# The decay products over all 128 rows of PE, with zeros in the selection matrix, in a three-stage kernel

## The chip, the cores and the metric

The kernel runs on one core of one Trainium2 chip. The metric is the device time of one execution in microseconds, lower is better. The median of three timed runs of the kernel before is 510.32 us (509.98 to 510.88). One execution was taken by the hardware profiler.

## The reference

Three stages follow one another: a chunked linear attention over 4 batches of 8 heads with 768 steps, then two layers of 8 experts that send each of 3072 tokens to one expert. The change touches the attention alone. Cut to what matters there:

```python
for c in range(nc):                       # chunks of the sequence
    la = log_a[:, :, sl]
    cum = np.cumsum(la, axis=-1)
    L = np.exp(cum[:, :, :, None] - cum[:, :, None, :]) * causal
    M = np.einsum('bhin,bhjn->bhij', Cc, Bc) * L
    y_intra = np.einsum('bhij,bhjd->bhid', M, xc)
    y_inter = np.einsum('bhin,bhnd->bhid', Cc, state) * np.exp(cum)[..., None]
    y[:, :, sl] = y_intra + y_inter
    state = decay_full * state + np.sum(Bx * decay_from_j, axis=2)
...
x = _moe_ref(x=x, **moe_kwargs)
return _moe2_ref(x=x, **moe2_kwargs)
```

`L` holds the decay products: for steps i and j of a chunk, the product of all `a` between them.

## The kernel before

The attention is cut into chunks of 64 steps (12 in a sequence) and eight quads `q`, a quad being four heads of a batch. Every engine has its own queue and runs it in order; the queues are filled in the order in which the program is written, and waits are put in wherever an instruction reads or overwrites what another engine writes or reads.

The decay products are made by a scan on DVE (line 580) along a row of `a`. The row has to stand on all 64 partitions of a head's chunk, so PE spreads it: `decay_piece(b, g, v)` (line 570) multiplies a selection matrix `selA` (ones in the row of the head, zeros elsewhere) by `asp`, which holds `a` of all 32 batch-and-head rows. To keep the precision of 32 bits `a` is split in a high part (rows 0 to 31) and the rest (rows 32 to 63), and the product adds both. Two matmuls of 256 columns, called a pair here, fill one PSUM tile `ab`. The products use only rows 0 to 63 of PE (`tile_position=(0, 0)`). Rows 64 to 127 of the same two tiles serve another purpose: there `asp` holds the running product from a chunk's start, and `selA` in its first 512 columns a selection for it, which `quad_p` (line 685) multiplies on rows 64 to 127 of PE (tile `pp`, 384 columns, one matmul for each quad).

`asp` is written in two steps. Rows 0 to 63 are written near the start (`a_part`, lines 861 to 864). Rows 64 to 127 are written in `chunk_start` (line 897): DVE scans `ac` (line 903), ACT casts the result into `asp[64:128]` (line 907), and a later DVE subtraction puts the rest into `asp[96:128]` (line 913). Between those two the program has `pend.intra(1)`.

A generator (`filler`, line 618) gives out the steps in a fixed order: for each pair of chunks `k` the product `cb` of C and B (line 603, two 32-bit matmuls of 256 columns, each recorded as two), and then one `decay_piece`. `psA`, the PSUM pool that `ab` and `cb` share, has two buffers. While batch 0 is worked on, `need` (line 653) puts a matmul `pw` on zeros of 512 columns (line 651) behind each step; these are the fillers. `quad_intra` (line 711) makes the `y` products with 64-column weights from the finished masks `mb` (line 610, DVE).

At the program's start POOL clears the buffers that SP's loads fill in part (`cw`, which holds the three `ctm`, and `xbd`); SP issues the loads in order, so a load that waits for a clear holds those behind it.

Of the kernel before, what the change touches and what calls it, by code (L numbers as in the profile page):

```python
# [9 lines left out]
F32 = mybir.dt.float32  # L10
F32R = mybir.dt.float32r
# [8 lines left out]
NB, NH, S, HD, NS = 4, 8, 768, 32, 16  # L20
NTOK, D, E, F = NB * S, 256, 8, 1024
CH = 64
# [14 lines left out]
def ssm_moe_moe_kernel(  # L37
# [20 lines left out]
    pe, dve, act, pool, sp = nc.tensor, nc.vector, nc.scalar, nc.gpsimd, nc.sync  # L58
# [461 lines left out]
    with ExitStack() as actx:  # L520
# [3 lines left out]
        ab = actx.enter_context(tc.tile_pool(name="ab", bufs=1))  # L524
# [45 lines left out]
        def decay_piece(b, g, v):  # L570

            if v == 0:
                lts[b, g] = fil_p.tile([128, 4, 4, CH], F32, tag="lt", name=f"lt{b}_{g}", bufs=3)
            p = psA.tile([128, 512], F32, tag="a", name=f"ab{b}_{g}_{v}")
            for k in range(2):
                u = 4 * b + 2 * v + k
                pe.matmul(p[:, 256 * k:256 * k + 256], lhsT=selA[0:64, 128 * u:128 * u + 128],  # L577
                          rhs=asp[0:64, 256 * g:256 * g + 256], start=True, stop=True,
                          tile_position=(0, 0))
            dve.tensor_tensor_scan(  # L580
                lts[b, g][:, 2 * v:2 * v + 2].rearrange("p u c i -> p (u c i)"), p,
                ipat[:].rearrange("p c i -> p (c i)"), 0.0, op0=ALU.mult, op1=ALU.add,
            )
            if v == 1:
                lt = lts[b, g]
                for hq in range(2):
                    m = au.tile([128, 2, 4, 80], F32, tag=f"mb{hq}", name=f"mb{b}_{g}_{hq}",
                                bufs=5 + hq)
                    mbs[2 * b + hq, g] = m
                    us_ = slice(2 * hq, 2 * hq + 2)  # L590
                    pool.tensor_tensor(  # L591
                        m[:, :, :, 64:80], brs[b][:, us_, 4 * g:4 * g + 4],
                        lt[:, us_, :, CH - 1:CH].to_broadcast([128, 2, 4, NS]), ALU.mult,
                    )
# [23 lines left out]
        def filler():  # L618
            for b in range(NB):
                if b == 0:  # L620
                    for v in range(2):
                        decay_piece(0, 0, v)
                        yield
                for k in range(6):
                    yield from cb_steps(b, k)
                    fpos[b] = 2 * k + 1
                    yield
                    gb, gg = divmod(3 * b + k // 2 + 1, 3)
                    if gb < NB:
                        decay_piece(gb, gg, k % 2)  # L630
                        yield
# [14 lines left out]
        def warm(n):  # L646

            nwarm[0] += 1
            p = psC.tile([128, 512], F32, tag="c", name=f"pw{nwarm[0]}")
            for _ in range(n):  # L650
                pe.matmul(p, lhsT=wz[:, :128], rhs=wz, start=True, stop=True)

        def need(b, c):
            while fpos.get(b, -1) < c:
                if next(fil_gen, "end") == "end":
                    return
                if b == 0:
                    warm(1)
# [26 lines left out]
        def quad_p(q):  # L685

            b, hq = divmod(q, 2)
            p = psC.tile([128, 512], F32, tag="c", name=f"pp{q}")
            pe.matmul(p[:, :384], lhsT=selA[64:128, 128 * b:128 * b + 128],
                      rhs=asp[64:128, 384 * hq:384 * hq + 384], start=True, stop=True,  # L690
                      tile_position=(64, 0))
            pv = p[:, :384].rearrange("p (v i) -> p v i", i=CH)
            if q == NQ - 2:
                return pv
            t = au.tile([128, 6, CH], F32, tag="pt", name=f"pt{q}")
            act.copy(t, pv)
            return t
# [113 lines left out]
        def run(gen, n=None):  # L811
# [17 lines left out]
            out=ident, in_=ident, compare_op=ALU.not_equal, fill=1.0, base=0,  # L829
            pattern=[[-1, 128]], channel_multiplier=1,  # L830
        )
        pool.memset(ctm[0][:, :2], 0.0)
        pool.memset(ctm[1], 0.0)
        xbd = [ab.tile([128, NCH, 64], F32, name=f"xbd{i}") for i in range(4)]
# [11 lines left out]
        dve.tensor_reduce(idk, ident[:].rearrange("p (b k) -> p k b", k=32), axis=AX.X, op=ALU.add)  # L846
        hm = ab.tile([128, 2], F32, name="hm")
        dve.tensor_reduce(hm, idk[:].rearrange("p (h n) -> p h n", n=16), axis=AX.X, op=ALU.add)
        selA = ab.tile([128, 32 * CH], F32R, name="selA")
        asp = ab.tile([128, S], F32R, name="asp")  # L850

        def sel_part(b):
            hs = slice(8 * b, 8 * b + 8)
            act.copy(
                selA[0:64, 512 * b:512 * b + 512].rearrange("p (h j) -> p h j", j=CH),
                idk[0:64, hs].unsqueeze(2).to_broadcast([64, 8, CH]),
            )
# [9 lines left out]
        a_part(0, 256)  # L867
        a_part(256, S)
        sel_part(0)
        ipat = const.tile([128, 8, CH], F32, name="ipat")  # L870
        cxs = {0: load_cx(0), 1: load_cx(1)}
# [104 lines left out]
        pend = Quad(0)  # L976
        pend.intra(0)
        sel_part(1)
        halves[2] = expand_half(2, raws[2])
        xts[1] = expand_x(1, xcs[1], act.copy)  # L980
# [7 lines left out]
        for q in range(4):  # L988
# [2 lines left out]
        need(0, 7)  # L991
        pool.memset(cxb[0], 0.0)
        need(0, 11)
        act.copy(
            selA[64:128, :512].rearrange("p (h n) -> p h n", n=NS),
            idk[64:128].unsqueeze(2).to_broadcast([64, 32, NS]),
        )
        halves[3] = expand_half(3, raws[3])
# [15 lines left out]
        for b in range(2, NB):  # L1014
            sel_part(b)
# [11 lines left out]
        for q in range(1, NQ - 2):  # L1027
            b, hq = divmod(q, 2)
# [3 lines left out]
            if q == 1:  # L1032
                prefill(scr1, R1, [(C1P, C1T)], range(4))
                pts[0] = quad_p(0)
                for r in range(4):
                    quad_c(0, r)
                warm(2)
                fil(1)
                run(cs)
                warm(2)  # L1040
                pend.fb = quad_f(0)
            sx = quad_state(q - 1, pend.us, pend.fb)
            cur.intra(0)
            fil(1)
            pts[q] = quad_p(q)
            pend.ss = quad_transpose(q - 1, sx)
            fil(1)
# [46 lines left out]
        c6.intra(1)  # L1094
        run(router, 1)
        pts[q] = quad_p(q)
        run(router, 1)
        pend.ss = quad_transpose(q - 1, sx)
# [221 lines left out]
    for e in range(E):  # L1320
# [6 lines left out]
        for f in range(KF):  # L1327
# [3 lines left out]
            if nxr is not None and f in (4, 6):  # L1331
# [3 lines left out]
        n = nc.values_load(cnt2[0:1, e:e + 1], min_val=0, max_val=NTOK + NE,  # L1335
                           skip_runtime_bounds_check_because="counts of tokens")
# [80 lines left out]
```

## Time and profile before

| | us |
|---|---|
| median of three timed runs | 510.32 |
| the profiled execution, its own time | 506.59 |
| its span, first to last instruction | 504.9 |
| PE busy | 461.8 |
| DVE busy | 287.9 |
| ACT busy | 240.1 |
| POOL busy | 138.2 |
| attention and routing, up to the first expert's matmuls | about 143 |

Busy times are those of an engine's instructions in the profiled execution, whose span is 1.7 us shorter than its own time. PE's clock has two levels, 1.2 and 2.4 GHz; the granted clock of a stretch is a mean of the two, as a share of the higher one. PE is followed by its weight loads as an engine of its own (PEld), since these run beside matmuls. The start of a matmul is recorded, and its end is worked out by the profiler, so the distances between starts are the ones to read.

### The profile page before, as it was taken

How to read it: one execution, taken by the hardware profiler on the slowest of the kernel's cores; microseconds unless marked ns; L12 is line 12 of the kernel's file. 1: busy time of each engine (PE TensorE's matmuls, PEld its weight loads, DVE VectorE, ACT ScalarE, POOL GpSimd, SP SyncE). 2: the span in 40 equal slices, each digit the busy share in tenths (PEclk: the TensorE clock that was granted, in tenths of full speed). 3: DMA queues.
4: the chain of work that ended last, by engine and by line, in shares of the span. 5: the costliest groups of instructions: out<-in, count | busy, mean ns of one | idle time of the engine just before them, and what ended most of it. 6: DMA issues, size and time to landing. Idle time of an engine off the chain costs nothing.

```text
span 504.9 us, 8965 instructions
## 1 busy us (share of the span) xinstructions
PE 461.8 (91%) x3208; PEld 413.7 (82%) x3208; DVE 287.9 (57%) x681; ACT 240.1 (48%) x557; POOL 138.2 (27%) x210
## 2 busy tenths in 40 slices
PE   8889987988579999999999999879999999999992
PEld 3555755767569999999999999879999999999991
DVE  7877786877545836547373656533675367244330
ACT  5542443656435644637354465424566356344330
POOL 6334455156730021230303122411101210212011
PEclk9897998989959999999999999889999999999997
DMA  7257899785224535253443444260654564411000
GB/s 261 68 170 183 229 209 249 169 273 194 80 84 166 176 106 183 93 159 105 140 149 113 150 143 164 73 204 30 225 179 162 174 206 154 143 34 63 22 23 15
DMA packets 50226, 72.22 MB, mean 143 GB/s; under 512 B 23870, under 2 KB 36093, under 8 KB 49899
## 3 DMA queue, kind: packets, MB, share of 16 engines
q1 hardware_dynamic: 45595, 61.66, 41.3%
q0 software_dynamic: 4560, 9.70, 5.7%
q8 instruction: 34, 0.56, 0.5%
q14 instruction: 37, 0.30, 0.2%
HBM read 52.53 MB, written 19.74 MB: 143 GB/s over the span
## 4 chain that ended last, share of the span: by engine, by line
PE 47%; DMA 22%; issue 13%; DVE 9%; POOL 3%; ACT 2%; SPq 1%; POOLq 1%; another core or an unknown queue 0%; DVEq 0%; ACTq 0%
DMA out_dram<-os0n,idsn 13%; PE y1m L330 7%; PE y0m L330 7%; DMA out_dram<-os0n0a,idsn0a 7%; PE cb L603 3%; DVE lt L580 2%; PE h0m L308 2%; PE h1m L308 2%; PE h2m L308 2%; PE y L758 2%; PE h3m L308 2%; PE h6m L308 2%; PE h5m L308 2%; PE h7m L308 2%; PE h4m L308 2%
## 5 line engine op out<-in xcount | busy, mean ns | idle before, releaser
L218 POOL DMA_INDIRECT scr<-rows2m,idxm x31 | 31.4, 1014 | 128.7 <-DVE cum L215 105.3
L121 DVE TENSOR_TENSOR w0l<-raw,w0h 128x1024 fp32r<-128x1024 f32 x30 | 36.7, 1225 | 10.7 <-ACT w0h L120 10.7
L121 DVE TENSOR_TENSOR w1l<-raw,w1h 128x1024 fp32r<-128x1024 f32 x30 | 36.4, 1216 | 1.0 <-ACT w1h L120 1.0
L603 PE MATMUL cb<-cw,btt 128*128 128x256 f32 x96 | 31.6, 435 | 1.4 <-DVE mb L610 0.9
L437 POOL DMA_INDIRECT out_dram<-os0n,idsn x8 | 7.8, 969 | 89.1 <-ACT os0n L436 55.8
L218 POOL DMA_INDIRECT scr<-rows,idxa x24 | 26.3, 1094 | 20.3 <-DVE cum L215 10.3
L120 ACT CAST w1h<-raw 128x1024 fp32r<-128x1024 f32 x30 | 31.5, 1052 | 0.0
L120 ACT CAST w0h<-raw 128x1024 fp32r<-128x1024 f32 x30 | 31.2, 1042 | 0.0
L580 DVE TENSOR_TENSOR_SCAN lt<-ab,ipat 128x512 f32<-128x512 f32 x24 | 29.2, 1217 | 2.2 <-PE ab L577 2.0
L312 DVE SCALAR_TENSOR_TENSOR hln<-h0n,hhn 128x384 fp32r<-128x384 f32 (+1 forms) x8 | 4.2, 524 | 45.4 <-ACT hhn L311 41.5
L603 PEld LDWEIGHTS cb<-cw,btt 128*128 128x128 f32 x96 | 17.9, 209 | 9.2 <-issue 2.2
L610 DVE TENSOR_TENSOR mb<-cb,lt 128x256 f32<-128x256 f32 x48 | 18.0, 416 | 11.4 <-PE cb L603 9.4
L330 PE MATMUL y1m<-hhm,w1h 128*128 128x432 f32 (+1 forms) x64 | 23.0, 360 | 0.0
L330 PE MATMUL y0m<-hhm,w1h 128*128 128x432 f32 (+1 forms) x64 | 22.9, 358 | 0.0
L312 DVE SCALAR_TENSOR_TENSOR hlm<-h0m,hhm 128x432 fp32r<-128x432 f32 (+1 forms) x8 | 4.7, 586 | 31.4 <-ACT hhm L311 24.4
L330 PE MATMUL y0m<-hhm,w1l 128*128 128x432 f32 (+1 forms) x64 | 22.4, 350 | 0.0
L330 PE MATMUL y1m<-hhm,w1l 128*128 128x432 f32 (+1 forms) x64 | 22.3, 349 | 0.0
L330 PE MATMUL y0m<-hlm,w1h 128*128 128x432 f32 (+1 forms) x64 | 22.3, 348 | 0.0
L330 PE MATMUL y1m<-hlm,w1h 128*128 128x432 f32 (+1 forms) x64 | 22.3, 348 | 0.0
L591 POOL TENSOR_TENSOR mb<-brt,lt 128x128 f32<-128x128 f32 x24 | 10.5, 438 | 38.8 <-DVE lt L580 34.4
L715 PEld LDWEIGHTS y<-mb,xbd 128*64 128x64 f32 x384 | 14.8, 138 | 5.7 <-issue 2.0
L335 ACT COPY ytm<-y1m 128x432 f32<-128x432 f32 (+1 forms) x8 | 4.0, 502 | 31.8 <-PE y1m L330 31.8
(603 smaller groups left out, 1579.0 us busy)
## 6 DMA issues: line engine op xcount, KB each, us to landing
raw<-in_m2w_dram SPq DMA_DIRECT2D x32, 512.0 KB
raw<-in_m1w_dram SPq DMA_DIRECT2D x28, 512.0 KB
scr<-zrow SPq DMA_DIRECT2D x8, 448.9 KB
scr<-zrow SPq DMA_DIRECT2D x8, 399.0 KB
xrm<-scr SPq DMA_DIRECT2D x7, 448.9 KB
xrn<-scr SPq DMA_DIRECT2D x6, 399.0 KB
xbd<-in_xs__dram SPq DMA_DIRECT2D x24, 96.0 KB
scr<-zrow SPq DMA_DIRECT2D x8, 266.0 KB
```

What stands on the lines that cost most here:

```text
L120: act.copy(hi[:, sl], raw)
L121: dve.tensor_tensor(lo[:, sl], raw, hi[:, sl].bitcast(F32), ALU.subtract)
L218: i = pool.indirect_dma_start(out=scr[:], out_offset=bass.IndirectOffsetOnAxis(ap=idx[:pn, t, :], axis=0), in_=rows[:, t, :W], in_offset=None,
L308: pe.matmul(p[:, :n], lhsT=w[:, o:o + 128], rhs=x[:, kd, :n], start=(k == 0), stop=(k == 5))
L312: dve.scalar_tensor_tensor(hl[:, f, :n], p[:, :n], 0.0, hh[:, f, :n].bitcast(F32), op0=ALU.max, op1=ALU.subtract,)
L330: pe.matmul(p[:, :n], lhsT=w[:, o:o + 128], rhs=h[:, f, :n], start=(k == 0), stop=(k == 3 * KF - 1))
L580: dve.tensor_tensor_scan(lts[b, g][:, 2 * v:2 * v + 2].rearrange("p u c i -> p (u c i)"), p, ipat[:].rearrange("p c i -> p (c i)"), 0.0, o ...
L591: pool.tensor_tensor(m[:, :, :, 64:80], brs[b][:, us_, 4 * g:4 * g + 4], lt[:, us_, :, CH - 1:CH].to_broadcast([128, 2, 4, NS]), ALU.mult,)
L603: pe.matmul(p[:, cc], lhsT=btt[:, c].rearrange("p h j -> p (h j)"), rhs=ctt[:, :, c * CH:(c + 1) * CH], start=True, stop=True)
L610: dve.tensor_tensor(mbs[2 * b + hq, g][:, :, o:o + 2, :64].rearrange("p u c i -> p c u i"), p[:, :, us_, :], lts[b, g][:, us_, o:o + 2, :] ...
L715: pe.matmul(yps[g][64 * hs:64 * hs + 64, r * 80:r * 80 + 80], lhsT=xts[hs][:, c, :], rhs=mbs[q, c // 4][:, hs, c % 4, :], start=(r == 0), ...
L758: pe.matmul(yps[g][64 * hs:64 * hs + 64, :320].rearrange("p (c w) -> p c w", w=80)[:, :n, :64], lhsT=ss[:, g, 64 * hs:64 * hs + 64], rhs=c ...
```

## The change

The decay products and `pp` are no longer made on half of the rows of PE. The selection of `pp` moves out of `selA` into a tile of its own, `selP`, with zeros in rows 0 to 63. Rows 64 to 127 of `selA` become zeros, so that a product over all 128 rows has the same value. POOL clears those rows, and at the start also `asp[64:128]`, which is read before its values are written. The numbers of instructions on PE, DVE, ACT and SP stay as they were; POOL gets six clears more.

```diff
--- before.py
+++ after.py
@@ -574,9 +574,8 @@
             p = psA.tile([128, 512], F32, tag="a", name=f"ab{b}_{g}_{v}")
             for k in range(2):
                 u = 4 * b + 2 * v + k
-                pe.matmul(p[:, 256 * k:256 * k + 256], lhsT=selA[0:64, 128 * u:128 * u + 128],
-                          rhs=asp[0:64, 256 * g:256 * g + 256], start=True, stop=True,
-                          tile_position=(0, 0))
+                pe.matmul(p[:, 256 * k:256 * k + 256], lhsT=selA[:, 128 * u:128 * u + 128],
+                          rhs=asp[:, 256 * g:256 * g + 256], start=True, stop=True)
             dve.tensor_tensor_scan(
                 lts[b, g][:, 2 * v:2 * v + 2].rearrange("p u c i -> p (u c i)"), p,
                 ipat[:].rearrange("p c i -> p (c i)"), 0.0, op0=ALU.mult, op1=ALU.add,
@@ -686,9 +685,8 @@
 
             b, hq = divmod(q, 2)
             p = psC.tile([128, 512], F32, tag="c", name=f"pp{q}")
-            pe.matmul(p[:, :384], lhsT=selA[64:128, 128 * b:128 * b + 128],
-                      rhs=asp[64:128, 384 * hq:384 * hq + 384], start=True, stop=True,
-                      tile_position=(64, 0))
+            pe.matmul(p[:, :384], lhsT=selP[:, 128 * b:128 * b + 128],
+                      rhs=asp[:, 384 * hq:384 * hq + 384], start=True, stop=True)
             pv = p[:, :384].rearrange("p (v i) -> p v i", i=CH)
             if q == NQ - 2:
                 return pv
@@ -829,6 +827,10 @@
             out=ident, in_=ident, compare_op=ALU.not_equal, fill=1.0, base=0,
             pattern=[[-1, 128]], channel_multiplier=1,
         )
+        selA = ab.tile([128, 32 * CH], F32R, name="selA")
+        asp = ab.tile([128, S], F32R, name="asp")
+        pool.memset(selA[64:128, :512].bitcast(F32), 0.0)
+        pool.memset(asp[64:128].bitcast(F32), 0.0)
         pool.memset(ctm[0][:, :2], 0.0)
         pool.memset(ctm[1], 0.0)
         xbd = [ab.tile([128, NCH, 64], F32, name=f"xbd{i}") for i in range(4)]
@@ -846,11 +848,12 @@
         dve.tensor_reduce(idk, ident[:].rearrange("p (b k) -> p k b", k=32), axis=AX.X, op=ALU.add)
         hm = ab.tile([128, 2], F32, name="hm")
         dve.tensor_reduce(hm, idk[:].rearrange("p (h n) -> p h n", n=16), axis=AX.X, op=ALU.add)
-        selA = ab.tile([128, 32 * CH], F32R, name="selA")
-        asp = ab.tile([128, S], F32R, name="asp")
+        selP = ab.tile([128, 4 * 128], F32R, name="selP")
 
         def sel_part(b):
             hs = slice(8 * b, 8 * b + 8)
+            if b:
+                pool.memset(selA[64:128, 512 * b:512 * b + 512].bitcast(F32), 0.0)
             act.copy(
                 selA[0:64, 512 * b:512 * b + 512].rearrange("p (h j) -> p h j", j=CH),
                 idk[0:64, hs].unsqueeze(2).to_broadcast([64, 8, CH]),
@@ -991,8 +994,9 @@
         need(0, 7)
         pool.memset(cxb[0], 0.0)
         need(0, 11)
+        pool.memset(selP[0:64].bitcast(F32), 0.0)
         act.copy(
-            selA[64:128, :512].rearrange("p (h n) -> p h n", n=NS),
+            selP[64:128].rearrange("p (h n) -> p h n", n=NS),
             idk[64:128].unsqueeze(2).to_broadcast([64, 32, NS]),
         )
         halves[3] = expand_half(3, raws[3])
```

On PE, in batch 0 behind the first `y` products, stands the third decay piece (tile `ab_2_0`; `pw` is a filler, `cb_3` the product of chunk pair 3). Before:

```order
L715 MATMUL y_0_242<-mb_1_0_258,xbd_121 64x80
L577 MATMUL ab_2_0_307<-asp,selA 128x256 x2
L651 LDWEIGHTS wz
L651 MATMUL pw_311<-wz 128x512 [waits PE_49]
L603 MATMUL cb_3_313<-cw,btt_208 128x256 [waits DMAHW1_49,DMAHW2_49,DMAHW0_49,DMAHW3_49,DVE_49,PE_49]
```

And now:

```order
L713 MATMUL y_0_245<-mb_1_0_261,xbd_125 64x80
L577 MATMUL ab_2_0_311<-asp,selA 128x256 [waits Activation_49]
L577 MATMUL ab_2_0_311<-asp,selA 128x256
L650 LDWEIGHTS wz
L650 MATMUL pw_315<-wz 128x512 [waits PE_49]
L602 MATMUL cb_3_317<-cw,btt_211 128x256 [waits DMAHW1_49,DMAHW2_49,DMAHW0_49,DMAHW3_49,DVE_49,PE_49]
```

The order is the same, but the pair now waits for ACT, whose queue has these rows up to the cast into the upper half of `asp` (the last but one):

```order
L722 COPY us_243<-y_0_245 128x16x4
L857 CAST selA<-idk 64x512
L548 ACTIVATE btt_287<-btr_233,hm 128x6x64 x2
L667 COPY xbd_126<-xc_187 64x12x32 x2
L667 COPY xbd_127<-xc_187 64x12x32 x2
L985 CAST sel<-idk 64x1024
L910 CAST asp<-ac 64x768
L914 CAST fp<-fc 64x12
```

This queue is as it was before, and its first row still waits for the `y` product of PE that stands ahead of the pair.

On POOL, at the program's start, the queue was this:

```order
L828 AFFINE_SELECT ident<-ident 128x128
L832 MEMSET cw 128x768
L833 MEMSET cw 128x1536
L837 MEMSET xbd_120 128x768
L837 MEMSET xbd_121 128x768
```

And is now this:

```order
L826 AFFINE_SELECT ident<-ident 128x128
L832 MEMSET selA 64x512
L833 MEMSET asp 64x768
L834 MEMSET cw 128x768
L835 MEMSET cw 128x1536
L839 MEMSET xbd_124 128x768
L839 MEMSET xbd_125 128x768
```

Two clears stand ahead of those of `cw`, for which SP's loads wait.

## Rows read from the trace of the kernel before

**Rows 1.** The page's head and its row of granted clock, 40 slices of the span.

```profile
span 504.9 us, 8965 instructions
...
PEclk9897998989959999999999999889999999999997
```

**Rows 2.** Stretches: length, busy us of PE, PEld, DVE, ACT, POOL, clock, DMA.

```profile
21.00:24.00 3.00, 3.00 (x23) 1.71 (x22) 1.52 (x4) 0.23 (x3) 2.27 (x11) 0.66 0.00 0
...
37.00:44.00 7.00, 7.00 (x21) 4.02 (x22) 3.94 (x7) 2.49 (x7) 4.62 (x6) 0.54 0.69 172
...
62.00:85.00 23.00, 17.34 (x172) 11.92 (x173) 18.48 (x42) 9.97 (x35) 14.39 (x18) 0.99 1.03 223
...
143.00:505.00 362.00, 344.04 (x2281) 331.90 (x2281) 182.65 (x405) 172.54 (x341) 67.51 (x94) 0.97 0.39 126
```

**Rows 3.** Instructions of lines 577 and 689: count, ns min/median/max, first and last start.

```profile
L577 PE MATMUL ab<-asp,selA x48: 273/381/579, 6.0 to 89.9; 64*128 64x256 f32 x48
...
L689 PE MATMUL pp<-asp,selA x8: 435/440/442, 29.0 to 102.9; 64*128 64x384 f32 x8
```

**Rows 4.** Timeline of PE, 10.5 to 13: start us, us, what [idle before <-releaser].

```profile
10.54 0.38 PE L651 MATMUL pw<-wz 128*128 128x512 bf16 x1
...
10.76 0.59 PE L603 MATMUL cb<-cw,btt 128*128 128x256 f32 x2
...
11.84 0.38 PE L651 MATMUL pw<-wz 128*128 128x512 bf16 x1
12.15 0.50 PE L577 MATMUL ab<-asp,selA 64*128 64x256 f32 x2
12.58 0.39 PE L651 MATMUL pw<-wz 128*128 128x512 bf16 x1
```

**Rows 5.** Timeline of PE in the second expert layer, two neighbours.

```profile
357.56 0.28 PE L455 MATMUL o0n<-w1l,hhn 128*128 128x256 f32 x1
357.68 0.28 PE L455 MATMUL o0n<-w1h,hln 128*128 128x256 f32 x1
```

**Rows 6.** Timeline of all engines, the head of the program.

```profile
14.47 0.73 POOL L981 MEMSET d<- 64x768 f32 x1
...
15.16 0.50 PE L577 MATMUL ab<-asp,selA 64*128 64x256 f32 x2
...
15.27 0.23 ACT L724 COPY us<-y 128x64 f32<-128x64 f32 x1 [3.23 <-PE y L715]
...
19.50 0.72 PE L577 MATMUL ab<-asp,selA 64*128 64x256 f32 x2 [2.23 <-DVE lt L580]
...
20.19 0.83 ACT L907 CAST asp<-ac 64x768 fp32r<-64x768 f32 x1
...
22.94 0.76 DVE L610 TENSOR_TENSOR mb<-cb,lt 128x256 f32<-128x256 f32 x2 [1.45 <-PE cb L603]
...
23.73 0.96 DVE L913 TENSOR_TENSOR asp<-ac,asp 32x768 fp32r<-32x768 f32 x1
...
24.91 1.22 DVE L580 TENSOR_TENSOR_SCAN lt<-ab,ipat 128x512 f32<-128x512 f32 x1
...
28.91 0.41 POOL L591 TENSOR_TENSOR mb<-brt,lt 128x128 f32<-128x128 f32 x1 [2.28 <-DVE lt L580]
```

**Rows 7.** Pieces of the chain of waits: start us, us, what.

```profile
4.05 2.99 DMA btr<-in_bt_dram
...
8.42 1.10 PE cb L603 x4
...
36.80 0.72 PE ab L577 x2
...
39.53 0.72 PE ab L577 x2
...
54.54 0.43 PE ab L577 x2
...
57.04 0.43 PE ab L577 x2
```

## The prediction

> **What bounds the kernel now.** I read the page first: PE is the busy engine, and its granted clock is at full speed in most slices, with a few dips in the first third [rows 1]. The table of stretches splits that third: from 143 us on, the two expert stages keep PE busy for 344 of 362 us [rows 2], and no instruction of the change lies there. So the change is worth what it does before 143 us, and whatever it does there moves everything behind it. In that part the chain of waits changes engine every microsecond or so. In the stretch 62:85 DVE is busy for 18.5 of 23 us and PE for 17.3: neither is the bound alone, so a shorter matmul counts only where the chain runs through it.
>
> Next I read the decay products themselves: 48 matmuls of 64 rows by 256 columns in 24 pairs (`ab`, line 577) and 8 of 384 columns (`pp`, line 689) [rows 3]. The reader is to see the gaps around one pair [rows 4]. The filler matmul `pw` (512 columns) starts at 10.54 and its 128-row successor `cb` at 10.76, 0.22 us later: nothing is lost between them. At 11.84 another `pw` starts, but the pair behind it starts at 12.15, 0.31 later, and the matmul behind the pair only at 12.58. From the end of that `pw` (11.84 + 0.22 = 12.06) to 12.58 the pair holds PE for 0.52 us, 0.09 of it before its first weight load.
>
> Last I read the head of the program, where `asp` is written [rows 6]. Its upper half gets its value from ACT at 20.19 to 21.02 and its lower part of that from DVE at 23.73 to 24.69. The pair at 15.16 runs five microseconds before the first of these, since it reads only the lower half.
>
> **The change part by part.**
> *Full rows.* The nearest 128-row matmuls of the same type and width are those of the second expert layer, spaced 0.12 us [rows 5], weights loaded meanwhile. A pair would take 0.24 instead of 0.52 us between two 128-row neighbours: 0.28 saved. If its successor is a 64-column product `y`, the 0.09 us gap stays in front of that: 0.19 saved; behind a `y` it stays too: 0.1. Bounds: 0 (the gaps have another cause) and 0.28; I take the values by neighbour, since [rows 5] has the same shape. At half clock the chain has 0.72 us for a pair [rows 7], which becomes 4 x 0.12 = 0.47: 0.25 saved. A `pp` saves about 0.28 in the same way.
>
> On the path: the chain runs through the pairs at 36.80 and 39.53 (half clock, 2 x 0.25 = 0.5) and at 54.54 and 57.04 (before a `y` each, 2 x 0.19 = 0.38) [rows 7]; I also count the pair behind the `y` near 27 us (0.1) and the first `pp` (0.28). Pairs between 62 and 85 I cost at nothing: DVE covers them [rows 2]; if that cover were gone they would give 0.19 each. Gain: 1.26 us, with bounds 0 and 2.5.
>
> *The new wait on ACT.* `ab` now reads rows 64 to 127 of `asp` as well. Those rows meet zeros in the selection matrix, but they are read, so the third decay piece of batch 0, which the program emits after ACT's cast, waits for that cast. PE is in order: behind it are queued the fillers, the `cb` of chunk pair 3, the next pair and all `y` products. ACT works without a break from 15.27, when PE's first `y` releases it, to 21.02 [rows 6]. Of the two pairs queued ahead of that `y`, the one at 12.15 gets 0.28 shorter and the one before it, which waits for DVE, some 0.1, so the cast ends near 20.6 and PE starts the pair at 20.65 instead of 15.16. Before, PE did this pair early, and the following pair at 19.50.
>
> From 19.50 to DVE's product at 22.94 is one round (pair, filler, `cb`, filler, `cb`) [rows 6], at a granted clock of 0.66 in the stretch 21:24 [rows 2], that is, mostly at the lower level: 3.44 us. After the change two rounds must follow 20.65. PE will have stood idle from 15 to 20.65, longer than the idle time of 2.2 us ahead of 19.50, after which the granted clock fell to half, so the first round is at half clock too: DVE's product of its `cb` at 24.0, PE free one filler later, near 24.2. The second round takes some 3.0 us if still at half clock (3.44 less 0.25 for the pair and less its load, now hidden), to 27.2, or at full clock about 1.8, where DVE's scan of 1.22 us ends last (26.0). Against 22.94 that is 3.1 to 4.3 us later; I take the middle, 3.6, since the clock should come back somewhere inside the round.
>
> *The new wait on DVE.* The pair of batch 1 now waits for DVE's subtraction at 23.73. Before, the scan at 24.91 began 0.22 us after that subtraction; now a pair (0.50 us [rows 4]) and two semaphores lie between, 0.57: 0.35 more.
>
> *Memsets.* POOL clears 64x512 and 64x768 ahead of the zeroes that SP's `cw` loads wait for: a clear of 64x768 takes 0.73 [rows 6], so about 1.2 us in all. SP is in order; every load behind, from `cw` to the second `btr` at 4.05, is issued 1.2 later. The chain passes through that `btr` to the `cb` at 8.42 [rows 7], but that `cb` needs only the first half of batch 0; the loads it needs are issued before 4.05, and even landing in the 2.99 us of that `btr` they are there at 7.0, 8.2 after the change. So I cost this at nothing, 0.4 at most if the landing is late. The clear of the next part of `selA` (about 0.5) delays the one of `d` at 14.47, and so DVE's scan of `ac`, by 0.5 less what the earlier `cb` gives; DVE would then wait for PE until 21 anyway. The later three clears, 1.5 us together, stand where POOL waits for DVE (2.28 us ahead of 28.91) [rows 6].
>
> *Sum.* 3.6 + 0.35 - 1.26 = +2.7 us. The profiled execution took 506.59 (span 504.9) and would take 509.3. The three timed runs have a median of 510.32, 3.7 above it; I put the change on that median: **513.0 us**.
>
> **The rivals.**
> *Not slower: PE is the bound at every pair.* Then all savings count: 8 pairs at 0.28, 13 at 0.19, 3 at 0.1 and 8 `pp` at 0.28, together 7.2, against 3.95 at the head: -3.2, 507.1 us. It decides if more than 4 us of the 7.2 lie on the path. The chain speaks against it: of its pieces from 60 to 76 us most are DVE's and ACT's, and DVE is the busier engine of 62:85. Chance 0.09.
>
> *The clock comes back sooner.* In 37:44 PE is busy all the time at a granted 0.54 of full speed [rows 2], that is, it is at 1.2 GHz for nearly all of it. Two pairs lie there with their gaps. If the denser stream, or the moved idle times, bring 2.4 GHz back half way, 3.4 us shrink to 1.7: 513.0 - 1.7 = 511.3 us. For it: clock dips follow idle stretches, and these move by 3 us against whatever grants it. Against: the idle time before the stretch (PE waiting for ACT) is still there. Chance 0.16.
>
> *The change does not do what it says: the gaps stay.* If the 0.52 us belong to the mix of types in the queue and not to the 64 rows, nothing is gained: +3.95, 514.3 us. For it: each pair stands between other types. Against: `pw` to `cb` also changes type, with no gap. Chance 0.13. The Trainium skill ("TensorE: Matmul & The Clock Gate", Part 3, The mechanism) states that a weight load overlaps running matmuls only when it is for another row group; by that rule full-row loads would be exposed and the full rows would gain nothing, as in this rival. The trace differs: full-row matmuls follow each other in 0.12 us, no more than their 256 columns nearly need, with a load for each [rows 5], so the load is hidden.
>
> **How the numbers follow.** Forecast (new waits at the head, gains on the chain only): 0.62, its own range 511.6 to 514.4 from the bounds 3.1 and 4.3 and the gain of 0.7 to 2. Rivals 0.09, 0.16, 0.13. The range runs from 509.8 (clock rival with more gain) to 515.0 (gaps stay, second round at half clock). A measurement of this kernel can tell about 0.2%, 1.0 us, from no change. Faster than 509.3: 0.10, the first rival and a little of the second. Within: 0.17, the rest of the second and the low tail of the forecast. Slower: 0.73.
>
> **What would show it.** In the changed kernel PE's third pair should start near 20.6 to 21, released by ACT's cast, and PE be idle before it; the granted clock should be half there. DVE's subtraction into `asp` should start 3 to 4 us later than 23.73 and the pair behind it should wait for it. A pair between 128-row neighbours should hold PE 0.24 us, and the stretches after 62 us should run at the old pace, shifted. The prediction is wrong if the third pair does not wait, if ACT's cast comes earlier, or if the 60 us behind the head win back more than 2.5 us.

## The result and the profile after

The changed kernel takes **511.68 us** (median of 20 executions, 509.5 to 516.04), the kernel before 507.83 us (20 executions, 502.28 to 513.13; the three behind the prediction's 510.32 us are among them). The ratio is **1.0099, 95% interval 1.0075 to 1.0124**: 5.0 us slower (3.8 to 6.3). That ratio leaves out executions more than 1.5% above the fastest of their kernel, which takes the five slowest of before and none of after; over all twenty of each the medians are 3.85 us apart. The prediction was 513.0 us, range 509.8 to 515.0, with a chance of 0.73 for slower. It holds, but its median of before, 510.32 us, came from three executions and was 2.5 us above that of twenty. The forecast difference was +2.7 us; the measured one is +3.9 to +5.0. So the sum was too small, and the sections below say where.

Single executions of one kernel differ by up to 11 us, so a profile gives a mechanism and not a total. The profiled execution of after took 513.56 us, 1.9 above its median, that of before 506.59, 1.2 below.

The page's head and its row of granted clock, after (to be held against [rows 1]):

```profile
span 511.9 us, 8968 instructions
...
PEclk9799999979978999999999999999999999999997
```

The span is 7.0 us longer. Of the 40 slices, of 12.6 to 12.8 us each, the clock is lower in the second, the ninth and the thirteenth, and higher in the fourth, the seventh, the twelfth, the 26th and the 27th. The stretches of [rows 2], after (length, busy us of PE, PEld, DVE, ACT, POOL, clock, DMA share, GB/s):

```profile
21.00:24.00 3.00, 1.49 (x5) 1.22 (x6) 0.65 (x1) 1.64 (x3) 0.00 (x0) 0.50 0.00 0
37.00:44.00 7.00, 4.28 (x33) 2.83 (x33) 5.91 (x13) 2.51 (x7) 3.11 (x7) 1.00 0.73 221
62.00:85.00 23.00, 16.23 (x163) 12.68 (x161) 15.11 (x38) 10.20 (x36) 12.55 (x17) 1.00 0.90 208
143.00:505.00 362.00, 342.77 (x2285) 329.73 (x2285) 184.32 (x419) 173.26 (x342) 70.62 (x99) 0.98 0.40 128
```

In 21:24 PE is busy for 1.5 of 3 us at half clock, where it was busy all the time: that is the new wait. In 37:44 the clock is 1.00, not 0.54: the half-clock stretch of before is not there in this execution.

One full-row pair on PE's timeline, after (start us, us, what), against [rows 4]:

```profile
12.20 0.38 PE L650 MATMUL pw<-wz 128*128 128x512 bf16 x1
12.20 0.41 PEld L577 LDWEIGHTS ab<-asp,selA 128*128 128x128 f32 x2
12.22 0.59 PE L577 MATMUL ab<-asp,selA 128*128 128x256 f32 x2
12.66 0.39 PE L650 MATMUL pw<-wz 128*128 128x512 bf16 x1
```

The pair's first weights are loaded at 12.20, while the `pw` of 0.22 us runs (to 12.42), and the next `pw` starts at 12.66. The pair holds PE for 0.24 us; before it was 0.52. Here the change does what it says. PE's busy time falls from 461.8 to 454.4 us, but the missing half-clock stretch is part of that, so it does not measure the pairs.

The head of the program, timeline of all engines, after, against [rows 6] (in brackets the idle time before and what ended it):

```profile
8.87 1.10 PE L602 MATMUL cb<-cw,btt 128*128 128x256 f32 x4 [1.19 <-POOL half L840]
...
15.62 0.23 ACT L722 COPY us<-y 128x64 f32<-128x64 f32 x1 [2.38 <-PE y L713]
...
17.45 1.12 ACT L548 ACTIVATE btt<-btr,hm 128x384 f32<-128x384 f32 x2 [0.97 <-DMA btr<-in_bt_dram]
...
21.63 0.83 ACT L910 CAST asp<-ac 64x768 fp32r<-64x768 f32 x1
...
22.51 0.80 PE L577 MATMUL ab<-asp,selA 128*128 128x256 f32 x2 [6.93 <-ACT asp L910]
...
28.19 0.76 DVE L609 TENSOR_TENSOR mb<-cb,lt 128x256 f32<-128x256 f32 x2 [0.25 <-PE cb L602]
...
28.98 0.95 DVE L916 TENSOR_TENSOR asp<-ac,asp 32x768 fp32r<-32x768 f32 x1
...
29.98 0.50 PE L577 MATMUL ab<-asp,selA 128*128 128x256 f32 x2 [0.86 <-DVE asp L916]
...
30.52 1.22 DVE L579 TENSOR_TENSOR_SCAN lt<-ab,ipat 128x512 f32<-128x512 f32 x1 [0.40 <-PE ab L577]
```

PE's third pair (22.51) waits 6.93 us for ACT's cast, the pair of batch 1 (29.98) for DVE's subtraction. DVE's product comes at 28.19 instead of 22.94, 5.25 us later.

Two views show what the profile of before does not have. The groups of waits, after (us in total, times, longest):

```profile
PE y L713 <- DMA xbd<-in_xs__dram: 7.0, 6, 1.6
```

And pieces of the chain of waits, after (start us, us, what):

```profile
65.82 3.04 DMA xbd<-in_xs__dram
...
78.65 2.73 DMA xbd<-in_xs__dram
...
100.27 4.80 DMA xbd<-in_xs__dram
```

PE waits six times for loads of `xbd`. The 5.25 us at the head had shrunk to 2.5 at 47 us (DVE's product at 46.48, before at 43.94), and grew to 7.1 at ACT's first copy of `us` for the seventh quad (106.60 instead of 99.47). From that copy to the end of the span before needs 405.4 us and after 405.3, so the 7.0 us between the two profiles are all there by then. The prediction has no such step.

### The profile page after: what moved, and what is told of

It is laid out like the page before. It is cut to its first block, busy times and chain, and to the rows that moved or that the text cites. A ratio compares the mean times of both kernels' runs of the same rounds, so it can differ in the third digit from the quotient of the medians.

```text
span 511.9 us, 8968 instructions
## 1 busy us (share of the span) xinstructions
PE 454.4 (89%) x3207; PEld 411.3 (80%) x3208; DVE 287.9 (56%) x681; ACT 240.7 (47%) x557; POOL 143.6 (28%) x216
## 4 chain that ended last, share of the span: by engine, by line
PE 42%; DMA 26%; issue 15%; DVE 6%; POOL 4%; ACT 3%; SPq 1%; POOLq 1%; another core or an unknown queue 0%; DVEq 0%; ACTq 0%
DMA out_dram<-os0n,idsn 12%; PE y0m L330 7%; DMA out_dram<-os0n0a,idsn0a 7%; PE y1m L330 7%; PE cb L602 3%; DMA xrm<-scr 2%; PE y L756 2%; DMA xbd<-in_xs__dram 2%; PE h0m L308 2%; PE y L713 2%; PE h6m L308 2%; PE h7m L308 2%; PE h1m L308 2%; PE h2m L308 2%; POOL scr L218 2%
## 5 line engine op out<-in xcount | busy, mean ns | idle before, releaser
L121 DVE TENSOR_TENSOR w0l<-raw,w0h 128x1024 fp32r<-128x1024 f32 x30 | 36.8, 1225 | 10.5 <-ACT w0h L120 10.5
L602 PE MATMUL cb<-cw,btt 128*128 128x256 f32 x96 | 29.3, 408 | 4.2 <-DVE mb L609 1.3
L713 PE MATMUL y<-mb,xbd 128*64 128x80 f32 x384 | 20.5, 251 | 7.2 <-DMA xbd<-in_xs__dram 7.0
L713 PEld LDWEIGHTS y<-mb,xbd 128*64 128x64 f32 x384 | 17.1, 147 | 11.7 <-DMA xbd<-in_xs__dram 5.2
L602 PEld LDWEIGHTS cb<-cw,btt 128*128 128x128 f32 x96 | 16.6, 195 | 11.2 <-PE y L756 3.5
L609 DVE TENSOR_TENSOR mb<-cb,lt 128x256 f32<-128x256 f32 x48 | 18.0, 417 | 12.8 <-PE cb L602 9.0
L577 PE MATMUL ab<-asp,selA 128*128 128x256 f32 x48 | 13.2, 361 | 9.3 <-ACT asp L910 6.9
```

Source lines behind the costliest of these rows:

```text
L121: dve.tensor_tensor(lo[:, sl], raw, hi[:, sl].bitcast(F32), ALU.subtract)
L577: pe.matmul(p[:, 256 * k:256 * k + 256], lhsT=selA[:, 128 * u:128 * u + 128], rhs=asp[:, 256 * g:256 * g + 256], start=True, stop=True)
L602: pe.matmul(p[:, cc], lhsT=btt[:, c].rearrange("p h j -> p (h j)"), rhs=ctt[:, :, c * CH:(c + 1) * CH], start=True, stop=True)
L609: dve.tensor_tensor(mbs[2 * b + hq, g][:, :, o:o + 2, :64].rearrange("p u c i -> p c u i"), p[:, :, us_, :], lts[b, g][:, us_, o:o + 2, :] ...
L713: pe.matmul(yps[g][64 * hs:64 * hs + 64, r * 80:r * 80 + 80], lhsT=xts[hs][:, c, :], rhs=mbs[q, c // 4][:, hs, c % 4, :], start=(r == 0), ...
```

## The experiments

In each table of edits the ratio is to the kernel before, executed on the same chip beside it. *wait*, *pre_after* and *early_after* have six executions each, the others twelve. The theories at the start: **A**, the new waits at the head are the loss, the clears a small part; **B**, the clears are the loss; **C**, the waits are, and the full rows bring nothing.

### The parts of the change one by one

*half*: the clears stay, the products go back to half rows.

```diff
-  pe.matmul(..., lhsT=selA[:, ...], rhs=asp[:, ...], start=True, stop=True)
+  pe.matmul(..., lhsT=selA[0:64, ...], rhs=asp[0:64, ...], ..., tile_position=(0, 0))
-  pe.matmul(..., lhsT=selP[:, ...], rhs=asp[:, ...], start=True, stop=True)
+  pe.matmul(..., lhsT=selP[64:128, ...], rhs=asp[64:128, ...], ..., tile_position=(64, 0))
```

> The changed kernel with both kinds of product put back on half of the rows (ab on rows 0 to 63, pp on rows 64 to 127); the clears and the separate selection tile of the change stay. It measures the clears alone. Theory A (the head's new waits are the loss, the clears a small part of it): 0.4 to 1.5 us over the kernel before, DVE's product at 22.94 no later than 24.4. Rival B (the clears, through the loads of SP that they delay, are the whole loss): 3 to 4 us over the kernel before. Rival C (the waits cost all, the full rows bring nothing): as A here.

*wait*: full rows only in the three pairs that have to wait, all else as in *half*. *late*: half rows in these three, all else as in the change.

```diff
+  if (b, g, v) not in ((0, 2, 0), (0, 2, 1), (1, 0, 0)):
+      pe.matmul(..., lhsT=selA[0:64, ...], rhs=asp[0:64, ...], ..., tile_position=(0, 0))
+  else:
+      pe.matmul(..., lhsT=selA[:, ...], rhs=asp[:, ...], start=True, stop=True)
```

This is the edit in *wait*; *late* has `in` for `not in`.

> The changed kernel with full rows only in the three pairs that now read the upper half of asp before or just as it is written (third and fourth chunk piece of batch 0's last group, first of batch 1); the other 21 pairs and all pp on half rows. It has the clears and the new waits and next to none of the gain. Theory A: slower than the changed kernel by the gain of the full rows, 1.3 to 3 us, so 5 to 7 us over the kernel before. Rival B: 3 to 4 us over the kernel before, as the kernel 'half'. Rival C (full rows bring nothing on the path): the same as the changed kernel, about 3.9 us over the kernel before.

> The changed kernel with only those three pairs back on half rows: all other pairs and all pp on full rows, so that no pair waits for ACT's cast or DVE's subtraction; the clears stay. Theory A: the clears cost 0.4 to 1.5 us and the full rows give back 1.3 to 3 us: 2.5 us faster to 0.2 us slower than the kernel before, and the head's DVE product near 23.5 to 24. Rival B: as the changed kernel, 3 to 4 us over the kernel before. Rival C: 0.4 to 1.5 us over the kernel before, as the kernel 'half'.

*sep*: all on full rows, the chunk values in a tile of their own.

```diff
-  act.copy(asp[hi], ac[hi])
+  act.copy(asq[hi], ac[hi])
-  dve.tensor_tensor(asp[96:128], ac[96:128], asp[96:128].bitcast(F32), ALU.subtract)
+  dve.tensor_tensor(asq[96:128], ac[96:128], asq[96:128].bitcast(F32), ALU.subtract)
-  rhs=asp[:, 384 * hq:384 * hq + 384]      (pp)
+  rhs=asq[:, 384 * hq:384 * hq + 384]
+  pool.memset(asq[0:64].bitcast(F32), 0.0)
...
-  d1 = ab.tile([128, 12, CH], ...)
+  d1 = ab.tile([128, S], F32, tag="yT", ..., bufs=4)
```

The last two lines move the tile `d1` into the buffers of `yT`, here and in the kernels built on *sep*; what that alone does was not measured.

> The changed kernel with all products on full rows, but the chunk part of asp in a tile of its own (asq, which pp reads), so that the upper half of asp holds zeros that nothing overwrites: the waits go without any pair going back to half rows. One more clear of 64x768 stands on POOL, behind the head. Theory A: within 0.7 us of the kernel 'late', on either side of it. Rival B: as the changed kernel. Rival C: as the kernel 'half'.

| kernel | clears | new waits | full rows | ratio (95%) | us |
|---|---|---|---|---|---|
| half | yes | no | none | 1.0031 (1.0000 to 1.0062) | +1.6 |
| wait | yes | yes | 3 pairs | 1.0163 (1.0119 to 1.0207) | +8.3 |
| the change | yes | yes | all | 1.0099 (1.0075 to 1.0124) | +5.0 |
| late | yes | no | all but 3 pairs | 1.0031 (1.0000 to 1.0061) | +1.6 |
| sep | yes | no | all | 1.0036 (1.0008 to 1.0063) | +1.8 |

Taking the waits away (the change to *sep* or *late*) removes 3.2 to 3.4 us, and adding them to *half* costs 6.7; in these comparisons the intervals do not overlap. So the waits are the larger part of the loss, and **B** falls: *wait* has the same clears as *half*. The clears' 1.6 us is at the edge of what can be told from nothing. What the full rows give depends on the rest: from *wait* to the change 3.3 us less (intervals just overlap), from *half* to *late* nothing. A had 1.3 to 3 us for both. So A is right on the waits, but *late*, and with it *sep*, came out as **C** gave them, level with *half*; only *wait* against the change speaks against C.

The traces show where a gain arises and where it goes. Behind the head the change wins back 3.6 us of DVE's delay (5.8 at its product at 31.83, 2.2 at 62.73), and 2.4 of them lie between two neighbouring products: 39.57 and 43.94 in before, 44.48 and 46.48 in after. That is the stretch 37:44, where before runs at half clock. Its granted clock is 0.54 in before, 0.53 in *pre_before* (below), 0.76 in *half* and 0.82 in *wait*, and 1.00 in the profiles of all nine kernels with most pairs on full rows; but it is 1.00 in *early_before* (below) too, on half rows. So full rows go with an earlier return of the full clock, and it is not shown that they alone bring it. *late* has that gain and loses it: its product at 57.57 is 2.3 us ahead of *half* (59.83), then PE waits 1.31 and 1.06 us for loads of `xbd` and runs at 0.53 to 0.62 of full speed from 63 to 67 us, and its product at 67.17 is 1.0 behind *half* (66.18).

The head in *wait*, timeline:

```profile
20.64 0.83 ACT L916 CAST asp<-ac 64x768 fp32r<-64x768 f32 x1
...
21.52 0.79 PE L582 MATMUL ab<-asp,selA 128*128 128x256 f32 x2 [5.84 <-ACT asp L916]
...
27.00 0.76 DVE L614 TENSOR_TENSOR mb<-cb,lt 128x256 f32<-128x256 f32 x2 [0.37 <-PE cb L607]
...
28.80 0.51 PE L582 MATMUL ab<-asp,selA 128*128 128x256 f32 x2 [0.87 <-DVE asp L922]
```

and in *half*:

```profile
8.87 1.10 PE L603 MATMUL cb<-cw,btt 128*128 128x256 f32 x4 [1.46 <-POOL half L842]
...
23.60 0.76 DVE L610 TENSOR_TENSOR mb<-cb,lt 128x256 f32<-128x256 f32 x2 [1.43 <-PE cb L603]
```

DVE's product is at 22.94 before, 23.60 with the clears, 27.00 with clears and waits: the new wait on ACT costs 3.4 us at this place and the clears 0.66. The cast starts at 20.64 in both. The 21.63 of after has 0.97 us of waiting for a `btr` load on ACT, which *half*, *wait*, *late* and *pre_after* (below, with the same head as the change) do not show; so it need not be in every execution.

### Who passes the delay on: the transfers

In *sep* DVE's product for the last chunks of the sixth quad comes at 94.54, 3.41 us ahead of before (97.95), but ACT's first copy of `us` for the seventh quad at 99.17, only 0.30 ahead. PE's timeline in *sep* between them:

```profile
96.90 0.32 PE L713 MATMUL y<-mb,xbd 128*64 128x80 f32 x2 [1.49 <-DMA xbd<-in_xs__dram]
97.78 3.43 PE L713 MATMUL y<-mb,xbd 128*64 128x80 f32 x46 [0.56 <-DMA xbd<-in_xs__dram]
```

A lead in computing ends here in waits for `xbd`: they hold 2.05 of the 3.11 us lost, and behind them PE runs at half clock (0.50 in 98:101). But such waits do not tell a slow kernel from a fast one: in one profile each they come to 7.0 us in the change, 6.8 in *late*, 6.9 in *sep*, 4.2 in *wait* and 1.2 in *half*. SP's queue in before, from one `cw` load to the first load of expert weights, and the same two rows of after:

```profile
39.56 1.74 SPq L541 DMA_DIRECT2D cw<-in_ct_dram  x4
...
102.31 0.90 SPq L86 DMA_DIRECT2D cw<-in_m1w_dram  x2
```

```profile
43.51 2.92 SPq L541 DMA_DIRECT2D cw<-in_ct_dram  x4
...
109.08 0.91 SPq L86 DMA_DIRECT2D cw<-in_m1w_dram  x2
```

Before needs 62.8 us between them, after 65.6, *half* 64.1, *sep* 64.6. These are not transfers alone: between 39 and 110 us SP itself waits for other engines for 13.6 us in before, 14.2 in after, 9.4 in *half* and 12.0 in *sep*. SP also writes zero rows (`scr<-zrow`, line 263), 8.9 MB between 30 and 97 us in before. This gives **theory D**: from 30 to 110 us the transfers are a bound of their own. **Rival E**: the chain of PE, DVE and ACT is the bound, and the transfers only end late.

*pre_before, pre_after, pre_sep*: the zero rows of three experts (2.0 MB) behind the first weight loads.

```diff
-  prefill(scr2, R2, [...], ((0, 1), (2, 3, 4), (5, 6), (7,))[q - 2])
+  if q < 4:
+      prefill(scr2, R2, [...], ((0, 1), (2, 3, 4))[q - 2])
...
   wload(7)
+  prefill(scr2, R2, [...], (5, 6, 7))
```

> The kernel before with one thing moved: the zero rows that SP writes into scr2 for experts 5 to 7 (2.0 MB of transfers) are queued behind the first-stage weight loads at 117 us, not between 70 and 97 us. Theory D (from 30 to 110 us the transfers of SP's queue are a bound of their own, which passes the head's delay on and swallows savings of PE): the DMA share in 85:100 falls from 0.83; this kernel has no wait of PE for xbd in its profile, so it gains 0 to 2 us. Rival E (the chain of PE, DVE and ACT is the bound there, the transfers only happen to end late): within 0.5 us of the kernel before, or 1 to 2 us slower, since the moved writes meet the scatters at 117 to 139 us.

> The changed kernel with the same move of the zero rows of experts 5 to 7. Theory D: the waits of PE for xbd after 85 us (2.2 us in the changed kernel) go, and with them the loss between DVE's product at 101.8 and ACT's copy at 106.6; 2 to 4 us faster than the changed kernel, so 1 to 3 us over the kernel before. Rival E: as the changed kernel, 4 to 6 us over the kernel before.

> The kernel 'sep' (full rows, no new waits) with the same move. In the profile of 'sep' DVE's products ran 3.4 us ahead of the kernel before at 95 us, and lost it by 99 us to waits for xbd. Theory D: the lead is kept: 2 to 4 us faster than 'sep', 1 to 3 us under the kernel before. Rival E: as 'sep', 0.4 to 3 us over the kernel before.

Measured: *pre_before* 1.0054 (1.0021 to 1.0086), *pre_after* 1.0127 (1.0084 to 1.0170), *pre_sep* 1.0065 (1.0031 to 1.0100): no faster than their counterparts, the first slower than the kernel before by 1.1 to 4.4 us. D's times are missed. The stretches 85:100 and 115:143 show where, first before, then *pre_before*:

```profile
85.00:100.00 15.00, 14.37 (x165) 11.23 (x164) 10.49 (x27) 7.48 (x33) 2.18 (x3) 0.90 0.83 206
...
115.00:143.00 28.00, 18.84 (x148) 16.31 (x146) 17.30 (x79) 13.81 (x47) 17.68 (x20) 0.93 0.41 135
```

```profile
85.00:100.00 15.00, 13.64 (x173) 10.43 (x172) 12.19 (x38) 8.70 (x35) 2.18 (x3) 1.00 0.61 112
...
115.00:143.00 28.00, 17.31 (x120) 15.51 (x118) 14.14 (x56) 11.56 (x36) 14.61 (x17) 0.81 0.72 191
```

And a row of DVE's timeline in *pre_before*:

```profile
131.37 0.18 DVE L206 TENSOR_REDUCE idxa<-psa 128x3 int32<-128x24 f32 x1 [5.35 <-DMA scr<-rows,idxa]
```

The DMA share falls from 0.83 to 0.61 at 85:100 and rises from 0.41 to 0.72 at 115:143, where the scatters of the tokens run; DVE then waits 5.35 us for one of them (5.33 in *pre_after*, 6.20 in *pre_sep*, no such wait in before). Up to 106 us D holds in the trace: ACT's copy of `us` for the seventh quad, 106.60 in after, comes at 101.06 in *pre_after*, and SP's stretch takes 60.9 us instead of 65.6. What was won there was lost, and more, behind it: from ACT's copy to the end of the span the three need 411 to 412 us, where before and after need 405.

*early_before, early_after, early_sep*: instead the first zero rows (1.8 MB) earlier, at 16 us, where SP would wait for PE.

```diff
   pool.memset(d1[64:128], 0.0)
+  pool.memset(zrow, 0.0)
+  pool.memset(zrow[:, :, 265:266], BIG)
...
   raws[3] = load_half(3)
+  prefill(scr1, R1, [(C1P, C1T)], range(4))
...
-  pool.memset(zrow, 0.0)
...
-  pool.memset(zrow[:, :, 265:266], BIG)
...
-  prefill(scr1, R1, [(C1P, C1T)], range(4))
```

> The kernel before with the zero rows of scr1 for experts 0 to 3 (1.8 MB) written earlier: SP issues them behind the load of half 3, at about 16 us, where it then waits for PE until 25.8 us and the transfers are at a share of 0.2 to 0.5, and not at 29.9 us; POOL clears zrow at about 15 us for that. Theory D (the transfers from 30 to 110 us are a bound of their own): at 210 GB/s 8.5 us of transfers leave that stretch and nothing is added at 113 to 140 us, where the moved writes of 'pre_before' were paid back. The kernel before is near balance there, so 1 to 3.5 us faster than it. Rival E (the later loss in the 'pre' kernels shows that the chain behind 110 us decides, whatever comes before): within 1 us of the kernel before.

> The changed kernel with the same earlier zero rows. Theory D: the waits of PE for xbd (7 us in the changed kernel) go almost wholly, what remains is the head's delay less the pairs' savings: DVE's products near 98 us as in 'pre_after' (1.6 us over the kernel before), and that lasts: 2.5 to 5 us faster than the changed kernel, 0 to 2.5 us over the kernel before. Rival E: as the changed kernel, 4 to 6 us over the kernel before.

> All products on full rows, the chunk part of asp in a tile of its own, the clears on DVE (the kernel 'sep_dve'), and the earlier zero rows. Theory D: the lead of 4 us that 'sep_dve' had over the kernel before at 95 us and lost to xbd by 99 us is kept: 2.5 to 5 us faster than the kernel before, and 1 to 3 us faster than 'early_before', which is what the full rows are worth where the transfers don't take it. If full rows bring nothing on the path: as 'early_before'. Rival E: as 'sep_dve', level with the kernel before.

*sep_dve*, the base of *early_sep*, is *sep* with the first two clears on DVE:

```diff
   dve.memset(ctm[0][:, 2:], 0.0)
+  dve.memset(selA[64:128, :512].bitcast(F32), 0.0)
+  dve.memset(asp[64:128].bitcast(F32), 0.0)
...
-  pool.memset(selA[64:128, :512].bitcast(F32), 0.0)
-  pool.memset(asp[64:128].bitcast(F32), 0.0)
```

> The kernel 'sep' with the two clears at the start (selA and asp, rows 64 to 127) made by DVE ahead of its first reductions, not by POOL ahead of the zeros that SP's loads wait for. SP's first cw load comes back from 3.45 to about 2.2 us, the head's product of DVE from 10.16 to about 9.7. Theory A (the clears cost 0 to 3 us, as in 'half'): 0.5 to 2 us faster than 'sep', so level with the kernel before. If the clears cost nothing: as 'sep'. If DVE is the tighter engine at the start (its first reductions come 1.2 us later, ACT's selA copy behind them): 0 to 1 us slower than 'sep'.

| kernel | ratio (95%) | us |
|---|---|---|
| sep_dve | 0.9997 (0.9966 to 1.0028) | -0.2 |
| early_before | 0.9994 (0.9972 to 1.0017) | -0.3 |
| early_after | 1.0090 (1.0057 to 1.0122) | +4.6 |
| early_sep | 0.9972 (0.9955 to 0.9989) | -1.4 |
| shift_sep | 0.9930 (0.9895 to 0.9964) | -3.5 |

With the clears on DVE the kernel is level with before, 2.0 us under *sep*, though the intervals overlap; its first `cb` on PE starts at 8.39, as before the change (8.42), and not at 8.87:

```profile
8.39 1.10 PE L602 MATMUL cb<-cw,btt 128*128 128x256 f32 x4 [1.05 <-DVE lt L579]
```

The earlier zero rows alone bring nothing to before or to after: D's 1 to 3.5 and 2.5 to 5 us are missed, and rival E's numbers are right. The time they free lies at 25:40, ahead of loads that PE releases, while 85:100 stays full (share 1.01 in *early_before*, 1.10 in *early_after*). *early_sep* is faster than before, by 1.4 us of the 2.5 to 5 that D gave, and 1.1 us under *early_before* with overlapping intervals. PE still waits there:

```profile
97.09 0.32 PE L713 MATMUL y<-mb,xbd 128*64 128x80 f32 x2 [3.03 <-DMA xbd<-in_xs__dram]
```

*shift_sep*: every later group of zero rows also one place up the queue, on top of *early_sep*.

```diff
   if q == 1:
+      prefill(scr1, R1, [(C1P, C1T)], range(4, 8))
       pts[0] = quad_p(0)
...
-  if q == 1:
-      prefill(scr1, R1, [(C1P, C1T)], range(4, 8))
-  else:
-      prefill(scr2, R2, [...], ((0, 1), (2, 3, 4), (5, 6), (7,))[q - 2])
+  if q < 5:
+      prefill(scr2, R2, [...], ((0, 1), (2, 3, 4), (5, 6), (7,))[q - 1])
```

> The kernel 'early_sep' with every later group of zero rows moved one place up SP's queue as well, so that the gap that 'early_sep' left idle at 30 to 38 us is used (its DMA share in 25:40 was 0.35) and 1.8 MB, 8.5 us at 210 GB/s, leave the stretch from 40 to 105 us. In all kernels so far with the whole of the writes in that stretch, SP needed 62 to 67 us from its cw load at 37 to 44 us to the first expert load at 101 to 109 us. Theory D (that stretch is bound by the transfers): here 56 to 61 us, PE's waits for xbd ahead of 95 us go, and 1 to 4 us faster than 'early_sep', 2.5 to 5.5 us under the kernel before. Rival E (the chain of PE, DVE and ACT needs that long in any case): within 1 us of 'early_sep'.

It is faster than the kernel before by 3.5 us (1.8 to 5.3), in the range that D gave, and the fastest ratio of all. It is 2.1 us under *early_sep*, with overlapping intervals, so between D (1 to 4 us) and E (within 1 us) this step alone does not decide. Its stretch 85:100 and its last waits for `xbd`:

```profile
85.00:100.00 15.00, 13.03 (x171) 10.63 (x170) 12.43 (x31) 7.88 (x34) 2.18 (x3) 1.00 0.56 111
```

```profile
74.06 0.32 PE L713 MATMUL y<-mb,xbd 128*64 128x80 f32 x2 [0.93 <-DMA xbd<-in_xs__dram]
...
76.20 1.25 PE L713 MATMUL y<-mb,xbd 128*64 128x80 f32 x14 [1.82 <-DMA xbd<-in_xs__dram]
```

The DMA share at 85:100 is down to 0.56, and behind 77 us PE waits for no `xbd`. But SP's stretch took 63.6 us and not 56 to 61: in this execution PE ran at half clock at 69 to 73 and 76 to 80 us, and SP's last loads (from 91.24 on) waited for PE. That execution took 508.8 us, 1.7 above the kernel's median and above the 506.59 of before, so its profile does not show the gain. The profiles suggest that the transfers and the chain of engines are close to each other in this part of the program, and that which one is late depends on where the clock falls in an execution. That a lead can end in waits for loads is shown in *sep*. *shift_sep* has fewer of these waits and is faster, but no kernel moved the later zero rows with the products on half rows, so it is not shown that it won what the waits had taken. How much of the change's loss they hold is not settled.

## Why the prediction was right, and what was mis-sized

- **The gaps go.** Predicted 0.24 us for a pair between 128-row neighbours, measured 0.24. The rival "the gaps stay" falls. So does, for these loads, the rule that the prediction weighed, the sentence in the Trainium skill, "TensorE: Matmul & The Clock Gate", Part 3, The mechanism, that a load overlaps running matmuls only when it is for another row group: here a full-row load begins at 12.20 beside a full-row matmul that runs to 12.42.
- **The new wait on ACT.** Predicted: pair at 20.65, DVE's product 3.6 us later (3.1 to 4.3). Measured: *wait* against *half*, 27.00 against 23.60, 3.4 us. The step was right. The start was later: 21.52 in *wait*, 22.51 in the profiled execution of after. ACT's first copy of `us` came 0.44 and 0.35 us later than in before, and not some 0.4 earlier, since the clears delay the first `cb` by 0.45. In after the shorter pair ahead of the `y` only leaves PE waiting (0.25 us for DVE at 13.30), and the 0.97 us for `btr` come on top. The prediction also took the clock to be at half behind the idle time: it was (0.50 in 21:24), but idle time alone does not settle it. At the same place PE sits idle for 2.7 us in *half* and 2.8 in *sep*, and 21:24 has 0.54 in the one and 1.00 in the other.
- **The new wait on DVE.** Predicted 0.35 us. After DVE's product, *wait* is 4.06 us behind before; at the product following that pair (30.65 against 26.05) it is 4.60, and *half* goes from 0.66 to 0.84. That leaves 0.36.
- **The clears: mis-sized.** Costed at nothing, 0.4 at most. The argument was that the loads of `cw` would still land by 8.2 us, ahead of the `cb` at 8.42. In after, *half*, *wait* and *late* that `cb` starts at 8.87, in *sep_dve* and *early_sep*, with the clears on DVE, at 8.39. At the end *half* measures 1.6 us (0.0 to 3.1). The profile names POOL's last clear (`half`) as what the `cb` waited for, but that ends at 8.07, 0.8 us ahead of it. The rows of the head point to the buffers: the `cb` is the third user of the two buffers of `psA` and needs the one that DVE's first scan reads, so it waits for that scan. Before, then after:

```profile
5.78 1.08 DVE L874 COPY ipat<-ident 64x512 f32<-64x512 f32 x2
6.96 1.22 DVE L580 TENSOR_TENSOR_SCAN lt<-ab,ipat 128x512 f32<-128x512 f32 x1
```

```profile
4.69 3.33 POOL L839 MEMSET xbd<- 128x768 f32 x4
5.90 1.44 DVE L877 COPY ipat<-ident 64x512 f32<-64x512 f32 x2
7.44 1.22 DVE L579 TENSOR_TENSOR_SCAN lt<-ab,ipat 128x512 f32<-128x512 f32 x1
```

The scan ends at 8.18 before and at 8.66 after, and the `cb` starts 0.24 and 0.21 us behind it. In all profiles with the clears on POOL the scan starts at 7.43 or 7.44, in all others at 6.96. It waits for DVE's copies into `ipat`, which take 1.4 to 1.6 us where POOL's clears of `xbd` run beside them (to 8.02) and 0.9 to 1.1 where these end by 6.1. So, by these rows, the clears cost 0.45 us at the first `cb` by moving POOL's later clears onto DVE's copies, and not through the loads that the prediction weighed. That the two slow each other is read from the rows and not tested by itself, and how 0.45 becomes 1.6 us at the end is not shown.

- **The gain: not as costed.** 1.26 us were predicted, most of it on four named pairs. With the waits in place the full rows gave back 3.3 us, without them nothing (*half* to *late*). Most of what the trace of after wins back is the half-clock stretch at 37:44, which is absent there, as in the second rival (chance 0.16). That rival's 511.3 us is nearer to the measured time than 513.0, but it meant a difference of +1.0, not +3.9 to +5.0. And the prediction named more than 2.5 us won back in the 60 us behind the head as a sign of being wrong: by 62 us the profiled execution of after had won back 3.0, and then lost it again, at the waits for `xbd`.
- **What the sum lacked.** The prediction had the DMA share of 1.03 in 62:85 in its rows [rows 2] and drew nothing from it; it took the stretches behind 62 us to run at the old pace. They did not: after is 2.2 us late at 62 us and 7.1 at 107. Between them PE waits 7.0 us for loads of `xbd`, for which the sum had no term. How much of the total they explain stays open, since *late* and *sep* wait as long and are 3 us faster.

So the sign and the main mechanism, the new waits at the head, hold. The terms for the clears and the gain do not, and what happens behind 62 us was not in the sum. That the time came within 1.3 us of the forecast is partly luck: its base was 2.5 us too high and its difference 1.2 (by the medians of all executions) to 2.3 (by the ratio) too low.

## What to carry to other kernels

A zero in a selection matrix does not take a row out of the dependences: reading rows that another engine fills later makes every reader wait for the writer, and an in-order engine makes everything behind it wait too. If the rows have to be read, give the zeros a tile that nobody writes afterwards and clear it where nothing is held up by it; with the clears on DVE (*sep_dve*) no loss was left to measure here (-0.2 us, -1.7 to 1.4). Before pricing savings on an engine, look whether the DMA share of the same stretch is near 1, since a lead can end in a wait for a load.

## What the runs showed of the hardware

SP's issues can stretch: a group of four issues of `xbd` took 2.7 to 2.8 us five times of six in before, and 4.2 and 5.5 us in two of the same places in after, of which SP's own waits are 0.8 and 0.9. And with 2.0 MB of plain writes beside the scatters one reader of a scatter waited 5.3 to 6.2 us in three kernels, where before had no such wait: writes that nobody waits for were not free there. At the head, DVE's two copies into `ipat` took 1.44 us beside POOL's clears and 1.08 where the clears end soon after they start, and POOL's clears of `xbd` took 0.87 us each instead of 0.74.
